# Attention with both heads of a pair in one weighted-sum batch, ahead of a mixture of experts and a dense layer

## The chip, the cores and the metric

The kernel runs on one core of a Trainium2 chip. A core has five engines that work side by side, each through its own queue in order: TensorE (matrix products; the trace lists its weight loads apart, as PEld), VectorE (DVE), ScalarE (ACT), GpSimd (POOL) and SyncE (SP), which here issues DMA transfers. The metric is the device time of one execution in microseconds (us); a figure for a kernel is the median of several runs.

## What is computed

Attention runs on two batches of eight heads, 768 tokens, 64 numbers per head. Queries and keys are given the nearest of 16 centroids of their head, and a query sees only keys of its own cluster. Its output goes through a mixture of eight experts (each token to the one expert with the largest logit) and then through a dense layer with a gated activation. Only attention and the two products that stand right behind it (the logits of the expert choice and of the output gate) are touched by the change.

```python
q_assign = argmax(einsum('bhsd,hcd->bhsc', q_n, c_n), -1)      # k_assign alike
mask = q_assign[:, :, :, None] == k_assign[:, :, None, :]
scores = where(mask, scale * q @ k.T, -1e9)
attn = exp(scores - max(scores, -1))
attn_out = (attn / (sum(attn, -1) + 1e-9)) @ v
x = attn_out.transpose(0, 2, 1, 3).reshape(B * S, H * D)
logits = x @ w_gate;  e_idx = argmax(logits, 1);  eom = sigmoid(x @ w_output_gate)
# x -> expert e_idx (relu(x @ w1[e]) @ w2[e], weighted) -> (g(x @ w_in)) @ w_out
```

## The kernel before

Attention is cut into eight units, a unit being a batch and a pair of heads; a unit has 12 steps, a step being 128 queries of one head against all 768 keys. So there are 96 steps, `i` in the loop, and r = 0 to 11 within a unit. All instructions are issued in an order written out by hand, so each engine takes its work in exactly the order of the program.

Pass `i` of the loop does, in this order: `prepare(i, True)` (pieces marked early); `emit_scores(i + 1)`, four TensorE products into one of two PSUM buffers (L419, L420) and the maximum on VectorE (L422); in every third pass one waiting output product, `ostage` (L474, L476); `prepare(i)`, other pieces of the next unit; one waiting weighted-sum batch, `weighted` (L459, L462, L464, L465); `emit_pt(i - 1)`, the transposes of the exponentials in two halves, each half with one PSUM buffer of its own, copied out by ScalarE (first half, L441) and by VectorE (second half, L443), with routing work spread between the halves; `emit_exp(i + 1)` on ScalarE (L428).

A weighted-sum batch covers one head and three steps: six blocks of 128 keys, each in two column groups of 32, even and odd blocks in different quarters of the array, so that four products run at once; every product is two instructions, as the numbers are 32 bits wide. Even and odd sums stay in two halves of the partitions, and the output product adds them: its moving matrix `wo` has, in each half, the unit matrix and that head's rows of the two gate matrices (80 columns). VectorE scales the product by the reciprocal of the sums of exponentials and puts it into `xw`. Batches are queued two passes after their last step; in a unit they run at r = 5, 8, 11 and at r = 2 of the next one, their output products one pass later. In all units but the last the steps go through one head and then through the other.

While a unit runs, the next one is prepared in nine pieces, at the passes that `plan_at` gives relative to the first step of the running unit (-3, -2, 0, 1, 3, 5, 6, 7, 8; for unit 1 the first two at 0): transposes of queries and keys, for each head (`pqk`, L256, in the one PSUM buffer that the batches use, too; high part by ScalarE, low part by VectorE, L260; six DMAs for the queries and six for the keys); cluster scores of both (`pcl`, L326, in the PSUM buffer of the output products) with a block transpose (L330) and the first maximum and comparisons on VectorE (L300 to L302); second maximum (L309); one-hots (L314); their block transpose (L334) with the rows of ones (L338, eight DMAs). Inputs of unit u + 2 are loaded at r = 9 of unit u - 1 (for unit 2 at pass 3). `setup_rest` fills `wo` ahead of the first pass. When the last output product of a batch's tokens is done, `route` picks the experts and scatters the rows; the expert stage follows.

Of the kernel before, what the change touches and what calls it, by code (L numbers as in the profile page):

```python
# [9 lines left out]
F32 = mybir.dt.float32  # L10
# [3 lines left out]
AF = mybir.ActivationFunctionType  # L14
ALU = mybir.AluOpType
# [4 lines left out]
B, H, S, D = 2, 8, 768, 64  # L20
C = 16
NT = B * S
DM = H * D
E = 8
DFF = 2048
T = S // 128
XW = 80
# [12 lines left out]
def tile_t(j):  # L40

    return 2 * (j % 3) + j // 3
# [3 lines left out]
def attention_moe_ffn(ctx: ExitStack, tc: tile.TileContext, q, k, v, centroids, w_gate, w_og, w1, w2, w_in, w_out, out):  # L46
    nc = tc.nc
# [6 lines left out]
    ident = const.tile([128, 128], F32, name="ident")  # L54
# [38 lines left out]
    at = ExitStack()  # L93
    ld = at.enter_context(tc.tile_pool(name="ld", reuse_waits="tile", bufs=2))
    one = at.enter_context(tc.tile_pool(name="one", reuse_waits="tile", bufs=1))
    stk = at.enter_context(tc.tile_pool(name="stk", reuse_waits="tile", bufs=2))
    pp = at.enter_context(tc.tile_pool(name="pp", reuse_waits="tile", bufs=4))
    ptp = at.enter_context(tc.tile_pool(name="ptp", reuse_waits="tile", bufs=2))
    xwp = at.enter_context(tc.tile_pool(name="xwp", reuse_waits="tile", bufs=1))
    xw = [xwp.tile([128, T, H, XW], F32, name=f"xw{b}") for b in range(B)]  # L100
    ps_s = at.enter_context(tc.tile_pool(name="ps_s", reuse_waits="tile", bufs=2, space=PSUM))
# [6 lines left out]
    oh_scale = one.tile([128, 1], F32, name="oh_scale")  # L108
    oh_bias = one.tile([128, 1], F32, name="oh_bias")
    nought = one.tile([128, 1], F32, name="nought")  # L110
    wo = one.tile([128, H, XW], F32, name="wo")
    tri = one.tile([128, 128], BF16, name="tri")
    ones = one.tile([128, 128], BF16, name="ones")

# [1 line left out]
    st = {}  # L116
# [74 lines left out]
    def setup_rest():  # L191

        blocks = f32(cblk).rearrange("p h (x r) c -> p h x (r c)", x=2)
        nc.gpsimd.tensor_tensor(cfull, blocks[:, :, 0], blocks[:, :, 1], op=ALU.add)
        nc.gpsimd.memset(oh_scale[0:64], 1.0)
        nc.gpsimd.memset(oh_scale[64:128], BIG)
        nc.gpsimd.memset(oh_bias[0:64], 0.0)
        nc.gpsimd.memset(oh_bias[64:128], -BIG)
        for r in range(2):
            rows = slice(64 * r, 64 * r + 64)  # L200
            nc.gpsimd.tensor_copy(wo[rows, :, 0:D], ident[rows, None, rows].to_broadcast([64, H, D]))
            nc.sync.dma_start(out=wo[rows, :, D:D + E], in_=w_gate.rearrange("(h d) e -> d h e", h=H))
            nc.sync.dma_start(out=wo[rows, :, D + E:XW], in_=w_og.rearrange("(h d) e -> d h e", h=H))
        t32 = one.tile([128, 128], F32, name="t32")
        nc.gpsimd.memset(t32, 1.0)
        nc.gpsimd.tensor_copy(ones, t32)
        nc.gpsimd.affine_select(out=t32, in_=t32, pattern=[[1, 128]], compare_op=ALU.is_gt, fill=0.0, base=0, channel_multiplier=-1)
        nc.gpsimd.tensor_copy(tri, t32)
        nc.gpsimd.tensor_copy(rev8, rev16[:, C - E:])
        ei = one.tile([128, E], I32, name="ei")  # L210
        nc.gpsimd.iota(ei, [[NT, E]], base=0, channel_multiplier=0)
        nc.gpsimd.tensor_copy(ebase, ei)
        nc.gpsimd.tensor_scalar(iota8, ebase, 1.0 / NT, None, op0=ALU.mult)
        for e in range(E):
# [22 lines left out]
    def prep_pieces(u):  # L237
# [148 lines left out]
        if u == 0:  # L386
# [3 lines left out]
            ]  # L390
        return [
            [transposes("q", 0)], [transposes("q", 1), stacks("q")], [transposes("k", 0)], [transposes("k", 1), stacks("k")],
            [], [scores, by_token, argmax_a], [argmax_b], [chosen], [by_cluster, rows_of_ones],
        ]


# [1 line left out]
    TAIL, WAITS = 3, (3, 2, 0)  # L398
    steps = [(u, h, j) for u in range(len(UNITS)) for h in range(2) for j in range(T)]

    steps[-2 * T:] = sorted(steps[-2 * T:], key=lambda s_: s_[2] // 3)
    NS = len(steps)
    live = {}

    def emit_scores(i):
        u, h, j = steps[i]
        d = st[u]
        L = live[i] = {}
        if j % 3 == 0:
            L["sm"] = pp.tile([128, 3], F32, name="sm", tag="sm")  # L410
            L["pT"] = ptp.tile([128, T, 384], F32, name="pT", tag="pT")
        else:
            for nm in ("sm", "pT"):
                L[nm] = live[i - 1][nm]
        sp = L["sp"] = ps_s.tile([128, 2, 512], F32, name="sp", tag="sp")
        cs = slice(j * 128, (j + 1) * 128)
        for n in range(2):
            ks = slice(384 * n, 384 * n + 384)
            nc.tensor.matmul(sp[:, n, :384], d["Q1"][:, h, cs], d["X"][:, h, ks], start=True, stop=False)  # L419
            nc.tensor.matmul(sp[:, n, :384], d["Q2"][:, h, cs], d["Z"][:, h, ks], start=False, stop=True)  # L420
        nm = L["nm"] = pp.tile([128, 1], F32, name="nm", tag="nm")
        nc.vector.tensor_reduce(nm, sp[:, :, :384], op=ALU.max, axis=AX.XY, negate=True)  # L422

    def emit_exp(i):
        L = live[i]
        j = steps[i][2]
        P = L["P"] = pp.tile([128, 2, 384], F32, name="P", tag="P")
        nc.scalar.activation(P, L["sp"][:, :, :384], AF.Exp, bias=L["nm"], accum_out=L["sm"][:, j % 3:j % 3 + 1])  # L428

    def emit_pt(i):  # L430
        L = live[i]
        j = steps[i][2]
        for n in range(2):
# [9 lines left out]
                nc.vector.tensor_copy(dst, src)  # L443
            advance(2)

    av = deque()
    ost = deque()

    def queue_av(i):
        u, h, j = steps[i]  # L450
        L = live[i]
        hold = {}

        def weighted():
            po = ps_a.tile([128, 512], F32, name="po", tag="po")
            for kt in range(T):
                for a in range(2):
                    g = 2 * (kt % 2) + a
                    nc.tensor.matmul(po[32 * g:32 * g + 32, :384], st[u]["v"][:, h, tile_t(kt), 32 * a:32 * a + 32],  # L459
                                     L["pT"][:, kt, :], start=kt < 2, stop=kt >= T - 2)  # L460
            oa = hold["oa"] = pp.tile([128, 384], F32, name="oa", tag="oa")
            nc.scalar.copy(oa, po[:, :384])  # L462
            rs = hold["rs"] = pp.tile([128, 3], F32, name="rs", tag="rs")
            nc.vector.tensor_scalar(rs, L["sm"], 1e-9, None, op0=ALU.add)  # L464
            nc.vector.reciprocal(rs, rs)  # L465
            ost.append(ostage)

        def ostage():
            b, pr = UNITS[u]
            hh = 2 * pr + h  # L470
            po = ps_m.tile([128, 512], F32, name="pox", tag="m")
            pv = po[:, :3 * XW].rearrange("p (r c) -> p r c", r=3)
            for r in range(3):
                nc.tensor.matmul(pv[:, r], hold["oa"][:, r * 128:(r + 1) * 128], wo[:, hh], start=True, stop=True)  # L474
            j0 = j - 2
            nc.vector.tensor_tensor(xw[b][:, j0:j0 + 3, hh, :], pv, hold["rs"][:, :, None].to_broadcast([128, 3, XW]), op=ALU.mult)  # L476
            if (hh, j0) == (H - 1, 0) and b == B - 1:
                routing.append(route(1))

        av.append(weighted)  # L480


# [181 lines left out]
            nc.vector.tensor_tensor(ci[:, b], t2, place[b], op=ALU.add)  # L664


    plan_at = {}
    for u in range(1, len(UNITS)):
        for n, r in enumerate((-3, -2, 0, 1, 3, 5, 6, 7, 8) if u > 1 else (0, 0, 0, 1, 3, 5, 6, 7, 8)):
            plan_at.setdefault((12 * (u - 1) + r, n == 6), []).append((u, n))  # L670
    pieces = {}

    def prepare(i, early=False):
        for u, n in plan_at.get((i, early), ()):
            if u not in pieces:
                pieces[u] = prep_pieces(u)
            for f in pieces[u][n]:
                f()

    with tc.manual_schedule():  # L680
# [14 lines left out]
        for i in range(NS + 2):  # L695
            nu, r = divmod(i + 3, 12)
            if i == 3 or r == 0 and nu + 2 < len(UNITS):
                load_unit(nu + 2)
            prepare(i, True)
            if i + 1 < NS:  # L700
                emit_scores(i + 1)
            tail = i >= NS - TAIL
            if (tail or i % 3 == 0) and ost:
                ost.popleft()()
            prepare(i)
            if i == 0:
# [527 lines left out]
```

## Time and profile before

| | us |
|---|---|
| median of 3 runs (744.11 to 746.38) | 746.01 |
| the profiled execution, time | 743.06 |
| its span, first to last instruction | 741.4 |
| TensorE busy in the span | 715.3 (96%) |
| VectorE busy | 476.1 (64%) |
| ScalarE busy | 391.6 (53%) |
| GpSimd busy | 221.4 (30%) |
| mean granted TensorE clock | 0.986 |

An engine's busy share is a mean over stages with different limits; attention is roughly the first 260 us of the span. Matrix products are pipelined, so their durations overlap: what one costs is read from start to start, not from its duration. The trace names what an idle engine waited for.

### The profile page before, as it was taken

To read this page: it belongs to the slowest core of one execution; us is meant where nothing else is said; L and a number is where in the kernel's file an instruction comes from. 1 tells how busy PE (TensorE), PEld (TensorE's weight loads), DVE (VectorE), ACT (ScalarE), POOL (GpSimd) and SP (SyncE) were. 2 spreads that over 40 slices of the span, in tenths; PEclk is the share of its full clock that TensorE was granted. 3 is DMA by queue.
4 is the path that set the end of the run, shared out by engine and by line. 5 is a ranking of instruction groups with operands and counts; after the bars stand their busy time and mean duration, and the time that the engine had idled before them with its cause. 6 is when DMAs were issued, how large, how long until landed. Compare 5 with 4: busy or idle time off the path is not lost.

```text
span 741.4 us, 12821 instructions
## 1 busy us (share of the span) xinstructions
PE 715.3 (96%) x4698; PEld 587.8 (79%) x4698; DVE 476.1 (64%) x918; ACT 391.6 (53%) x784; POOL 221.4 (30%) x161
## 2 busy tenths in 40 slices
PE   8999999999999978999989988999999999999996
PEld 5777777777777758999989888877888888888885
DVE  5878788788887761665667766787545656232322
ACT  3766666666666634557767676544434344222120
POOL 3000000000700035757778887222332212020202
PEclk8999999999999989999999999999999999999998
DMA  8765948538340049756676673232643211010101
GB/s 235 177 187 154 238 161 258 128 82 199 97 128 13 1 154 326 246 179 221 206 256 216 217 252 141 85 114 86 70 68 40 79 58 57 0 58 0 58 1 57
DMA packets 66243, 98.28 MB, mean 133 GB/s; under 512 B 9248, under 2 KB 44960, under 8 KB 66176
## 3 DMA queue, kind: packets, MB, share of 16 engines
q1 hardware_dynamic: 63872, 91.12, 43.1%
q0 software_dynamic: 2304, 6.30, 2.3%
q8 instruction: 38, 0.62, 0.4%
q14 instruction: 29, 0.24, 0.1%
HBM read 64.46 MB, written 12.59 MB: 104 GB/s over the span
## 4 chain that ended last, share of the span: by engine, by line
PE 27%; issue 16%; DVE 9%; ACT 5%; POOL 3%; DMA 2%; POOLq 0%; SPq 0%; ACTq 0%; DVEq 0%
PE ph L1064 3%; PE ph L1063 3%; PE ph L1062 3%; PE py L1156 3%; PE py L1155 3%; PE py L1154 3%; ACT w L786 2%; DMA xr<-xd 2%; DVE w L789 1%; PE py L886 1%; PE ph L886 1%; DVE ct L824 1%; DVE ph L893 1%; POOL out_dram L1164 1%; PE py L884 1%
## 5 line engine op out<-in xcount | busy, mean ns | idle before, releaser
L789 POOL TENSOR_TENSOR w<-raw,w 128x1024 fp32r<-128x1024 f32 x47 | 117.5, 2514 | 34.8 <-ACT w L786 32.0
L1139 DVE TENSOR_TENSOR sg<-ph,sg 128x512 f32<-128x512 f32 x48 | 33.2, 691 | 103.6 <-ACT sg L1138 103.2
L422 DVE TENSOR_REDUCE nm<-sp 128x1 f32<-128x768 f32 x96 | 91.3, 952 | 9.6 <-PE sp L420 8.4
L428 ACT ACTIVATE P<-sp,nm 128x768 f32<-128x768 f32 x96 | 87.1, 907 | 5.2 <-DVE nm L422 5.0
L1138 ACT ACTIVATE sg<-ph 128x512 f32<-128x512 f32 x48 | 28.7, 598 | 108.7 <-PE ph L1064 105.4
L836 POOL TENSOR_TENSOR w<-csq,w 128x512 fp32r<-128x512 f32 x32 | 43.5, 1360 | 137.0 <-ACT w L835 137.0
L436 PEld LDWEIGHTS pt<-ident,P 128*128 128x128 f32 x576 | 65.1, 143 | 21.3 <-issue 19.4
L436 PE MATMUL pt<-ident,P 128*128 128x128 f32 x576 | 81.2, 276 | 0.3 <-DVE pT L443 0.2
L1063 PE MATMUL ph<-ytl,w 128*128 128x512 f32 x192 | 76.1, 397 | 0.0
L1062 PE MATMUL ph<-yth,w 128*128 128x512 f32 x192 | 76.0, 396 | 0.0
L1064 PE MATMUL ph<-yth,w 128*128 128x512 f32 x192 | 75.6, 394 | 0.1
L1155 PE MATMUL py<-w,gh 128*128 128x512 f32 x192 | 75.3, 392 | 0.0
L1156 PE MATMUL py<-w,gl 128*128 128x512 f32 x192 | 75.2, 391 | 0.0
L1154 PE MATMUL py<-w,gh 128*128 128x512 f32 x192 | 74.9, 390 | 0.0
L419 PE MATMUL sp<-X,Q 128*128 128x384 f32 x192 | 73.5, 383 | 0.5 <-ACT P L428 0.4
L786 ACT CAST w<-raw 128x1024 fp32r<-128x1024 f32 x64 | 66.8, 1044 | 7.7 <-DMA raw<-in_moe_w_dram 7.6
L443 DVE COPY pT<-pt 128x384 f32<-128x384 f32 x96 | 52.8, 550 | 27.5 <-PE pt L436 27.1
L886 PE MATMUL py<-ht,w 128*128 128x480 f32 (+5 forms) x192 | 61.8, 373 | 7.0 <-DVE room L893 5.2
L459 PE MATMUL po<-pT,ld_v 128*32 128x384 f32 x768 | 68.4, 489 | 0.2 <-ACT pT L441 0.2
L420 PE MATMUL sp<-Z,Q 80*128 80x384 f32 x192 | 65.3, 340 | 0.5 <-DMA Z<-Hk 0.5
L886 PE MATMUL ph<-t,w 128*128 128x480 f32 (+5 forms) x192 | 61.1, 370 | 1.5 <-DVE ht L910 1.5
L585 POOL TENSOR_SCALAR xs<-xw,gate 128x512 f32<-128x512 f32 x6 | 9.9, 1643 | 174.6 <-DVE gate L567 174.2
(233 smaller groups left out, 1559.0 us busy)
## 6 DMA issues: line engine op xcount, KB each, us to landing
raw<-in_moe_w_dram SPq DMA_DIRECT2D x64, 512.0 KB, 4.0
raw<-in_moe_w_in_dram SPq DMA_DIRECT2D x16, 512.0 KB, 4.6
raw<-in_moe_w_out_dram SPq DMA_DIRECT2D x16, 512.0 KB, 3.6
Q<-Hq SPq DMA_DIRECT2D x32, 192.0 KB, 5.8
xd<-zrow SPq DMA_DIRECT2D x8, 768.0 KB, 6.9
ld_q<-in_q_dram SPq DMA_DIRECT2D x8, 384.0 KB, 3.6
ld_k<-in_k_dram SPq DMA_DIRECT2D x8, 384.0 KB, 4.9
ld_v<-in_v_dram SPq DMA_DIRECT2D x8, 384.0 KB, 6.1
```

The costliest lines, as they stand in the source:

```text
L422: nc.vector.tensor_reduce(nm, sp[:, :, :384], op=ALU.max, axis=AX.XY, negate=True)
L428: nc.scalar.activation(P, L["sp"][:, :, :384], AF.Exp, bias=L["nm"], accum_out=L["sm"][:, j % 3:j % 3 + 1])
L436: nc.tensor.transpose(pt[:, r * 128:(r + 1) * 128], L["P"][:, n, r * 128:(r + 1) * 128], ident)
L786: nc.scalar.copy(hi, r)
L789: (eng or nc.gpsimd).tensor_tensor(lo, r, f32(hi), op=ALU.subtract)
L886: nc.tensor.matmul(ps[:, :2 * n], w_hi, t, start=first, stop=False)
L1062: nc.tensor.matmul(ph, wa(key, 0, k, i), yth[:, k, cs], start=(k == 0), stop=False)
L1063: nc.tensor.matmul(ph, wa(key, 0, k, i), ytl[:, k, cs], start=False, stop=False)
L1064: nc.tensor.matmul(ph, wa(key, 1, k, i), yth[:, k, cs], start=False, stop=(k == 3))
L1154: nc.tensor.matmul(po[m], gh[:, ms], wb(key, 0, i), start=first, stop=False)
L1155: nc.tensor.matmul(po[m], gh[:, ms], wb(key, 1, i), start=False, stop=False)
L1156: nc.tensor.matmul(po[m], gl[:, ms], wb(key, 0, i), start=False, stop=last)
```

## The change

Units 1 to 7 go through the steps of both heads by thirds: three steps of head 0, three of head 1, three more of each (as the last unit did before). From unit 1 on, except for the second half of unit 7, one batch serves both heads: its four column groups hold two heads times two halves of the head's width, and all six blocks of keys add into the same groups. It is issued in two parts of three blocks, in two passes (r = 8 and 9, and r = 2 and 3 of the next unit), and gives one output product of 160 columns, with one copy, one reciprocal and one scaling for both heads; that product comes at r = 0 and 6. `wo` becomes wider, with zeros in the half of the other head; a second matrix `wl` keeps the old form for unit 0 and the end of unit 7, so that twelve small DMAs fill both in place of four. Four buffers hold transposed exponentials in place of two.

The plan of the pieces moves: for units 2 and on the cluster scores go from r = 5 to r = 2, the second maximum from 6 to 3, the one-hots from 7 to 3; for units 3 and on the queries are transposed at -2 and -1. For every unit the cluster scores now come behind the batch of their pass (before, ahead of it), and the block transpose of the one-hots goes with the one-hots.

```diff
-    ptp = at.enter_context(tc.tile_pool(name="ptp", reuse_waits="tile", bufs=2))
+    ptp = at.enter_context(tc.tile_pool(name="ptp", reuse_waits="tile", bufs=4))
-    wo = one.tile([128, H, XW], F32, name="wo")
+    wo = one.tile([128, H // 2, 2, XW], F32, name="wo")
+    wl = one.tile([128, 2, 2, XW], F32, name="wl")
+        nc.gpsimd.memset(wo, 0.0)
         for r in range(2):
             rows = slice(64 * r, 64 * r + 64)
-            nc.gpsimd.tensor_copy(wo[rows, :, 0:D], ident[rows, None, rows].to_broadcast([64, H, D]))
-            nc.sync.dma_start(out=wo[rows, :, D:D + E], in_=w_gate.rearrange("(h d) e -> d h e", h=H))
-            nc.sync.dma_start(out=wo[rows, :, D + E:XW], in_=w_og.rearrange("(h d) e -> d h e", h=H))
+            nc.gpsimd.tensor_copy(wo[rows, :, r, 0:D], ident[rows, None, rows].to_broadcast([64, H // 2, D]))
+            nc.gpsimd.tensor_copy(wl[rows, :, :, 0:D], ident[rows, None, None, rows].to_broadcast([64, 2, 2, D]))
+            for n, w in enumerate((w_gate, w_og)):
+                cs = slice(D + E * n, D + E * n + E)
+                by_head = w.rearrange("(p r d) e -> r d p e", r=2, d=D)
+                nc.sync.dma_start(out=wo[rows, :, r, cs], in_=by_head[r])
+                for m, d0 in enumerate((0, DM - 2 * D)):
+                    nc.sync.dma_start(out=wl[rows, m, :, cs], in_=w[d0:d0 + 2 * D].rearrange("(h d) e -> d h e", h=2))
-            [], [scores, by_token, argmax_a], [argmax_b], [chosen], [by_cluster, rows_of_ones],
+            [], [scores, by_token, argmax_a], [argmax_b], [chosen, by_cluster], [rows_of_ones],
-    steps[-2 * T:] = sorted(steps[-2 * T:], key=lambda s_: s_[2] // 3)
+    steps[2 * T:] = sorted(steps[2 * T:], key=lambda s_: (s_[0], s_[2] // 3))
+    KTS = (range(0, 3), range(3, T))
 ...
+        alone = u == 0 or i >= NS - T
+        heads = (h,) if alone else (0, 1)
+        if len(heads) == 2 and h == 0:
+            return
+        pts = [live[i]["pT"]] if alone else [live[i - 3]["pT"], live[i]["pT"]]
+        def products(kts):
 ...
+            for kt in kts:
+                for n, hh in enumerate(heads):
+                    for a in range(2):
+                        g = 2 * (kt % 2 if alone else n) + a
+                        nc.tensor.matmul(po[32 * g:32 * g + 32, :384], v_[:, hh, tile_t(kt), 32 * a:32 * a + 32],
+                                         pts[n][:, kt, :], start=kt < (2 if alone else 1), stop=kt >= T - (2 if alone else 1))
         def weighted():
+            products(KTS[-1] if not alone else range(T))
 ...
-                nc.tensor.matmul(pv[:, r], hold["oa"][:, r * 128:(r + 1) * 128], wo[:, hh], start=True, stop=True)
+                nc.tensor.matmul(pv[:, r], hold["oa"][:, r * 128:(r + 1) * 128], wl[:, int(u > 0), h] if alone else wo[:, pr], start=True, stop=True)
+        if not alone:
+            for kts in KTS[:-1]:
+                av.append(lambda kts=kts: products(kts))
         av.append(weighted)
+    PLAN = ((0, 0, 0, 1, 3, 5, 6, 7, 8), (-3, -2, 0, 1, 1, 2, 3, 3, 8), (-2, -1, 0, 1, 1, 2, 3, 3, 8))
-        for n, r in enumerate((-3, -2, 0, 1, 3, 5, 6, 7, 8) if u > 1 else (0, 0, 0, 1, 3, 5, 6, 7, 8)):
-            plan_at.setdefault((12 * (u - 1) + r, n == 6), []).append((u, n))
+        for n, r in enumerate(PLAN[min(u, 3) - 1]):
+            plan_at.setdefault((12 * (u - 1) + r, n == 6, n == 5), []).append((u, n))
                 if av:
                     av.popleft()()
+            prepare(i, False, True)
             if 0 <= i - 1 < NS:
                 emit_pt(i - 1)
```

## Rows read from the trace of the kernel before

**Rows 1.** Busy time by stretch: stretch, length, PE, PEld, DVE, ACT, POOL busy; clock, DMA

```profile
44.22:74.73 30.51, 30.51 (x271) 22.85 (x270) 24.91 (x48) 20.49 (x46) 0.00 (x0) 1.00 0.65 175
166.30:197.00 30.70, 30.70 (x275) 22.92 (x274) 26.91 (x68) 20.47 (x48) 8.36 (x6) 1.00 0.54 141
```

**Rows 2.** Timeline of TensorE, unit 1 from step 5: start, length, line, operation, count

```profile
59.71 0.52 PE L326 MATMUL pcl<-Hq,cfull 128*32 128x384 f32 x2
...
61.03 2.12 PE L459 MATMUL po<-pT,ld_v 128*32 128x384 f32 x24
63.08 0.87 PE L436 MATMUL pt<-ident,P 128*128 128x128 f32 x6
63.71 0.42 PE L419 MATMUL sp<-X,Q 128*128 128x384 f32 x1
...
64.51 0.79 PE L474 MATMUL pox<-wo,oa 128*128 128x80 f32 x6
65.13 0.82 PE L436 MATMUL pt<-ident,P 128*128 128x128 f32 x6
65.71 0.42 PE L419 MATMUL sp<-X,Q 128*128 128x384 f32 x1
...
67.09 0.44 PE L419 MATMUL sp<-X,Q 128*128 128x384 f32 x1
...
67.98 2.14 PE L459 MATMUL po<-pT,ld_v 128*32 128x384 f32 x24
```

**Rows 3.** Timeline of TensorE, unit 0: plain steps 2 to 4, and step 9

```profile
25.19 0.42 PE L419 MATMUL sp<-X,Q 128*128 128x384 f32 x1
...
28.29 0.44 PE L419 MATMUL sp<-X,Q 128*128 128x384 f32 x1
...
41.59 0.49 PE L256 MATMUL pqk<-ident,ld_q 128*128 128x128 f32 x3
```

**Rows 4.** Timeline of VectorE, unit 0, the maximum of the scores issued at 25.19

```profile
26.19 0.96 DVE L422 TENSOR_REDUCE nm<-sp 128x1 f32<-128x768 f32 x1
```

**Rows 5.** Timeline of TensorE, expert stage, first and last of thirteen products of 320 columns

```profile
304.17 0.31 PE L882 MATMUL py<-ht,w 128*128 128x320 f32 x1
...
305.93 0.31 PE L882 MATMUL ph<-t,w 128*128 128x320 f32 x1
```

**Rows 6.** Timeline of VectorE, unit 1, steps 5 to 8

```profile
61.28 0.58 DVE L330 STREAM_TRANSPOSE sc<-pcl 128x384 f32<-128x384 f32 x1 [0.43 <-PE pcl L326]
...
63.55 0.16 DVE L464 TENSOR_SCALAR rs<-sm 128x3 f32<-128x3 f32 x1
...
63.99 0.56 DVE L443 COPY pT<-pt 128x384 f32<-128x384 f32 x1
...
64.92 0.95 DVE L422 TENSOR_REDUCE nm<-sp 128x1 f32<-128x768 f32 x1
65.78 0.40 DVE L476 TENSOR_TENSOR xw<-pox,rs 128x240 f32<-128x240 f32 x1
66.10 0.55 DVE L443 COPY pT<-pt 128x384 f32<-128x384 f32 x1
...
67.65 0.55 DVE L314 TENSOR_TENSOR oh<-eq,m 128x384 bf16<-128x384 f32 x1
68.11 0.55 DVE L443 COPY pT<-pt 128x384 f32<-128x384 f32 x1
...
69.44 0.56 DVE L334 STREAM_TRANSPOSE oT<-oh 128x384 bf16<-128x384 bf16 x1
69.94 0.12 DVE L464 TENSOR_SCALAR rs<-sm 128x3 f32<-128x3 f32 x1
```

**Rows 7.** Timeline of SyncE's DMA queue, first load of a gate matrix, load of unit 2's queries

```profile
20.32 0.68 SPq L202 DMA_DIRECT2D wo<-in_moe_w_gate_dram  x1
...
33.51 0.76 SPq L127 DMA_DIRECT2D ld_q<-in_q_dram  x1
```

**Rows 8.** That load of queries by its tile: time from issue to landing

```profile
DMA to landing us min/median/max: 4.7/4.7/4.7
```

More of the change, by code (lines that the diff above doesn't have):

```diff
@@ L408, in emit_scores @@
         L = live[i] = {}
+        L["sm"] = live[i - 1]["sm"] if i % (6 if u else 3) else pp.tile([128, 2, 3], F32, name="sm", tag="sm")
         if j % 3 == 0:
-            L["sm"] = pp.tile([128, 3], F32, name="sm", tag="sm")
             L["pT"] = ptp.tile([128, T, 384], F32, name="pT", tag="pT")
         else:
-            for nm in ("sm", "pT"):
-                L[nm] = live[i - 1][nm]
+            L["pT"] = live[i - 1]["pT"]
         sp = L["sp"] = ps_s.tile([128, 2, 512], F32, name="sp", tag="sp")
@@ L425, in emit_exp @@
         L = live[i]
-        j = steps[i][2]
+        _, h, j = steps[i]
         P = L["P"] = pp.tile([128, 2, 384], F32, name="P", tag="P")
-        nc.scalar.activation(P, L["sp"][:, :, :384], AF.Exp, bias=L["nm"], accum_out=L["sm"][:, j % 3:j % 3 + 1])
+        nc.scalar.activation(P, L["sp"][:, :, :384], AF.Exp, bias=L["nm"], accum_out=L["sm"][:, h, j % 3:j % 3 + 1])
     def emit_pt(i):
@@ L450, in queue_av @@
         u, h, j = steps[i]
-        L = live[i]
-        hold = {}
-        def weighted():
[L455 to L460, printed above, removed]
-            oa = hold["oa"] = pp.tile([128, 384], F32, name="oa", tag="oa")
[L462 to L465, printed above, removed]
+        b, pr = UNITS[u]
@@ new lines, in queue_av @@
+        v_ = st[u]["v"]
+        j0 = j - 2
+        alone = u == 0 or i >= NS - T
[3 more added lines that the diff above has]
+        pts = [live[i]["pT"]] if alone else [live[i - 3]["pT"], live[i]["pT"]]
+        sums = live[i]["sm"]
+        hold = {}
+        def products(kts):
+            if "po" not in hold:
+                hold["po"] = ps_a.tile([128, 512], F32, name="po", tag="po")
+            po = hold["po"]
+            for kt in kts:
[4 more added lines that the diff above has]
+                                         pts[n][:, kt, :], start=kt < (2 if alone else 1), stop=kt >= T - (2 if alone else 1))
@@ L466, in weighted @@
+        def weighted():
+            products(KTS[-1] if not alone else range(T))
+            oa = hold["oa"] = pp.tile([128, 384], F32, name="oa", tag="oa")
+            nc.scalar.copy(oa, hold["po"][:, :384])
+            rs = hold["rs"] = pp.tile([128, 2, 3], F32, name="rs", tag="rs")
+            hs = slice(heads[0], heads[-1] + 1)
+            nc.vector.tensor_scalar(rs[:, hs], sums[:, hs], 1e-9, None, op0=ALU.add)
+            nc.vector.reciprocal(rs[:, hs], rs[:, hs])
             ost.append(ostage)
@@ L468, in ostage @@
         def ostage():
-            b, pr = UNITS[u]
-            hh = 2 * pr + h
+            n = len(heads)
+            hh = 2 * pr + heads[0]
             po = ps_m.tile([128, 512], F32, name="pox", tag="m")
-            pv = po[:, :3 * XW].rearrange("p (r c) -> p r c", r=3)
+            pv = po[:, :3 * n * XW].rearrange("p (r h c) -> p r h c", r=3, h=n)
             for r in range(3):
-                nc.tensor.matmul(pv[:, r], hold["oa"][:, r * 128:(r + 1) * 128], wo[:, hh], start=True, stop=True)
@@ L475, in ostage @@
-            j0 = j - 2
-            nc.vector.tensor_tensor(xw[b][:, j0:j0 + 3, hh, :], pv, hold["rs"][:, :, None].to_broadcast([128, 3, XW]), op=ALU.mult)
-            if (hh, j0) == (H - 1, 0) and b == B - 1:
+                nc.tensor.matmul(pv[:, r], hold["oa"][:, r * 128:(r + 1) * 128], wl[:, int(u > 0), h] if alone else wo[:, pr], start=True, stop=True)
+            scale = hold["rs"][:, heads[0]:heads[-1] + 1].rearrange("p h r -> p r h")
+            nc.vector.tensor_tensor(xw[b][:, j0:j0 + 3, hh:hh + n, :], pv, scale[:, :, :, None].to_broadcast([128, 3, n, XW]), op=ALU.mult)
@@ L478, in ostage @@
+            if (pr, j0) == (H // 2 - 1, 0) and b == B - 1:
                 routing.append(route(1))
+        if not alone:
+            for kts in KTS[:-1]:
+                av.append(lambda kts=kts: products(kts))
         av.append(weighted)
@@ L664, in place_ids, with prepare @@
             nc.vector.tensor_tensor(ci[:, b], t2, place[b], op=ALU.add)
+    PLAN = ((0, 0, 0, 1, 3, 5, 6, 7, 8), (-3, -2, 0, 1, 1, 2, 3, 3, 8), (-2, -1, 0, 1, 1, 2, 3, 3, 8))
     plan_at = {}
     for u in range(1, len(UNITS)):
-        for n, r in enumerate((-3, -2, 0, 1, 3, 5, 6, 7, 8) if u > 1 else (0, 0, 0, 1, 3, 5, 6, 7, 8)):
-            plan_at.setdefault((12 * (u - 1) + r, n == 6), []).append((u, n))
+        for n, r in enumerate(PLAN[min(u, 3) - 1]):
+            plan_at.setdefault((12 * (u - 1) + r, n == 6, n == 5), []).append((u, n))
     pieces = {}
-    def prepare(i, early=False):
-        for u, n in plan_at.get((i, early), ()):
+    def prepare(i, early=False, late=False):
+        for u, n in plan_at.get((i, early, late), ()):
             if u not in pieces:
```

## Prediction, on record before the changed kernel was run

> **What bounds the kernel now.** I read the busy times by stretch first. In a whole unit of attention TensorE is busy for all of its 30.51 us, VectorE for 24.91 and ScalarE for 20.49; GpSimd does nothing [rows 1]. So from unit 1 on, each microsecond taken from TensorE is gained, and each that TensorE must wait is lost, whatever the other engines' averages say. Next I read the order of TensorE and VectorE side by side, to get prices from start to start (in microseconds): transposes 0.58 (65.13 to 65.71), a plain step 1.38 (65.71 to 67.09), hence scores 0.80; scores ahead of a batch 0.89; a batch 2.05; transposes after it 0.63; an output product 0.62; cluster scores plus batch 3.37, of which the cluster scores are 1.32 [rows 2]. No wait stands in these rows: extra TensorE work lies between any two plain steps. Last I looked where TensorE does run plain steps in a row: in unit 0, where two of them take 28.29 - 25.19 = 3.10, not 2.76 [rows 3]. That is the loop scores, maximum, exponential, score buffer free again; the maximum starts 1.00 after the scores [rows 4], so from its start to the next scores but one it takes 2.10.
>
> **What is gained.** Thirteen pairs of batches (two in each of units 1 to 6, one in unit 7) become thirteen merged ones of the same 48 matmul instructions, so the sums cost the same: two parts of 2.05, two entries and two exits of the packed form, as before. The output product falls from twelve instructions of 80 columns to six of 160. At 80 columns they follow each other at 0.62 / 6 = 0.103 us [rows 2]. The expert matmuls stream 320 columns in one pass at 0.147 ((305.93 - 304.17) / 12), each with a weight load of its own [rows 5]; 160 columns in the two-pass format are as many passes of a column, so I take 6 x 0.147 = 0.88, against 2 x 0.62 = 1.24: 0.36 saved, times 13 = 4.7 us. Bounds: with the spacing still 0.103, 0.62 x 13 = 8.1; with no load hidden (0.103 + 0.147 / 2 = 0.177), 0.18 x 13 = 2.3. I take the middle, since the expert rows have the same load and stream.
>
> A rule that speaks against this: the Trainium skill (TensorE: Matmul & The Clock Gate, Back-to-back issue gap) gives an isolated matmul N / 2.4 + 2.5 ns, which for 160 column passes is 69 ns; by that alone columns set the price, the change moves no column, and nothing is saved. The same section says that in a stream with weight loads both set the spacing, and the measured 103 ns sides with that.
>
> Thirteen copies of the sum (ScalarE) and reciprocals and scalings of half the count (VectorE) go, too. I cost that at nothing: both engines have idle time in the average [rows 1].
>
> **What the moved preparation costs.** The cluster scores were in step 5, ahead of a batch, and their VectorE chain (block transpose, argmax) ran beside 2.05 us of batch; copies of step 5 came after both. For units 2 on they come in step 2, behind a part. Queued on VectorE behind the chain are the copy of the transposes of step 1, the second maximum, the maximum of step 4's scores, the one-hots, their block transpose, the reciprocals and the copy of step 2; TensorE's transposes wait for those copies, since each half has one buffer.
>
> A steady unit, from the start of step 2's scores (0): part at 0.89, cluster scores after it, transposes at 0.89 + 3.37 = 4.26, next scores 4.89, second part 5.78, transposes 7.83, scores 8.46, transposes 9.26, their second half 0.29 later, at 9.55. VectorE: the block transpose starts 1.57 after the cluster scores do [rows 2, 6], here about 4.4 (4.25 to 4.5). Four operations take 2.27 (61.28 to 63.55): copy at 6.67; copy and second maximum 0.93: maximum at 7.60; 0.86: one-hots at 8.46; 0.46: block transpose at 8.92; 0.50: reciprocals at 9.42; two of them 0.3: copy at 9.72, done at 9.72 + 0.55 = 10.27 [rows 6]. TensorE wants that buffer at 9.55 and gets it at 10.3: 0.74 lost. Next late is the maximum behind the copy (10.19): the scores two steps on can't start before 10.19 + 2.10 = 12.29, TensorE would be there at 10.3 + 0.29 + 1.38 = 11.97: 0.32. Together 1.06, and even without a late copy the two plain steps 4 and 5 cost 3.10 - 2.76 = 0.34.
>
> Unit 1 is worse: the batch in its step 2 is a whole one of unit 0, so step 3 has an output product (0.62) and no second part. By the same working the second halves wait 0.67 (step 3) and 1.69 (step 4), then 0.30 for the exponential, and steps 6 and 7 are plain, too (0.34): 3.0. Unit 0 keeps its plan, but its cluster scores also go behind the batch, in step 5, because the new third place takes every unit's: waits of 0.67 (step 6) and 0.73 (step 7, behind the second maximum, the maximum and the 0.32 of the scaling): 1.4. Unit 5 holds the routing of the first 768 tokens, 2.0 us more of VectorE [rows 1]; in between I take 1.2 of it (0 to 2.0): 2.25. Unit 6 ends with two plain steps, as unit 7 has no successor to prepare: 0.34; unit 7 has its own pair: 0.34.
>
> SyncE: twelve small loads of the gate weights in place of four. One takes 0.68 of its queue [rows 7], so the queue is 5.3 us later (4.8 to 7) by the load of unit 2's queries: issued at 33.51 + 5.3, landing 4.7 after that [rows 7, 8], at 43.5. TensorE wants them at 41.59 [rows 3], by then 1.4 later, 43.0: 0.5 lost (0 to 2.6). Behind it stand the other two loads and the ones' DMAs, wanted later. The memset of the wide weights is hidden on GpSimd, idle then; the extra buffers cost space only. Transposing the queries one step later puts four such steps in a row (10, 11, 0, 1), in each of which VectorE has 0.86 + 0.47 + 0.47 and TensorE 1.38 and a product of three; that lags by about 0.1 a step and an output product in step 0 makes up for it: nothing, up to 0.8 a unit where the one PSUM buffer of these transposes comes late. The tail: routing of the last batch's first half starts one step later, mostly beside the last batch: 0.3 (0 to 1).
>
> Sum: unit 0 1.4, load 0.5, unit 1 3.0, units 2, 3, 4 and 6 4 x 1.06 = 4.2, unit 5 2.25, 0.34 twice, tail 0.3: 12.3 lost; 4.7 gained; net 7.6 us slower. The profiled execution took 743.06 (span 741.4 and 1.66 around it), which gives 750.7; the median of the runs shown, 746.01, stands 2.95 above it, so I forecast **753.6 us** in those terms.
>
> **The rivals.** *The chain fits* (same): block transpose to copy is 5.9 us of VectorE against 5.2 of TensorE, so 0.7 less, by a shorter pipeline between operations than these rows show, and only the plain pairs cost (units 1 to 7: 0.34 x 7, another in unit 1, one at the end of 6), with the load 1.9 and the tail 0.3: 5.3 lost, 4.7 gained, 746.6 us. For it: the chain misses by under a microsecond. Against: units 0 and 1 miss by far more.
>
> *It does what it says* (faster): no wait, and the product at 4.7 to 8.1: 738 to 741.3 us. This needs the plain steps not to cost, and the rows of unit 0 say that they do. It decides against me if TensorE shows no wait in step 4 of a unit.
>
> *The backlog carries on* (slower still): four query and key steps lag, 0.8 in each of five units, 4 more: 757.6 us.
>
> *Columns set the product's price* (slower still): nothing gained, 746.0 + 12.3 = 758.3 us. The Trainium skill's isolated gap (above) is this rival's rule; the measured spacing speaks against it.
>
> **How the numbers follow.** Chances: forecast 0.60, carried backlog 0.12, no gain by columns 0.03, chain fits 0.15, as it says 0.10. The slower three make 0.75, the same 0.15, the faster 0.10 (0.3% is about what a measurement of this kernel can tell from no change). The range takes in the slower cases, with the price bounds, and the case of the chain that fits: 745.0 to 758.5; left out are the faster case and what lies beyond the ends. The slower cases' own range is 749 to 758.5.
>
> **What would show it.** Right: TensorE waits of 0.6 to 0.9 us in the second half of step 4's transposes, released by the copy to pT on VectorE, in units 2 to 6, of about 1.7 in unit 1; then one of 0.3 at scores, released by the exponential; a period of a steady unit of 30.5 - 0.7 + 1.1 = 30.9; output products of 160 columns at 0.15 us spacing; the load of unit 2's queries issued 5 us later. Wrong: a period under 30.2 us, TensorE busy without such waits, or a block transpose of the cluster scores that starts well before the transposes of its step.

## The result, and the profile after

| | before | after |
|---|---|---|
| median, us | 746.15 (744.11 to 746.38) | 753.23 (752.70 to 754.50) |
| the profiled execution, us (span) | 743.06 (741.4) | 754.50 (752.8) |
| TensorE busy, us (share) | 715.3 (96%) | 716.1 (95%) |
| VectorE busy, us (share) | 476.1 (64%) | 469.4 (62%) |

The changed kernel takes 1.0101 times as long as the kernel before, 95% interval 1.0084 to 1.0118: 7.1 us more by the medians (6.3 to 8.8 by the interval), where 7.6 were forecast. The median of the kernel before is now that of four runs; the forecast was put on that of the first three, 746.01. In the profiled executions TensorE is busy for 0.8 us more in a span that is 11.4 us longer: nearly all that is added is time in which it idles. The first view of after is the list of TensorE's waits in attention, from 33 to 268 us (us in total, times, longest):

```profile
PE pt L442 <- ACT pT L447: 5.5, 8, 1.1
PE pt L442 <- DVE pT L449: 1.2, 2, 0.8
PE sp L426 <- DMA Q<-ohT: 0.7, 1, 0.7
```

In after the scores stand at L425 and L426, the maximum at L428, the transposes at L442, their two copies at L447 (ScalarE) and L449 (VectorE), the batch at L477, the output product at L496, the cluster scores at L333, their block transpose at L337, the one-hots and theirs at L321 and L341. The busy times of a steady unit answer to [rows 1], from cluster scores to cluster scores:

```profile
90.14:120.98 30.84, 30.20 (x261) 21.84 (x256) 23.99 (x41) 19.70 (x43) 0.00 (x0) 1.00 0.69 199
```

TensorE is no longer busy throughout: 30.20 of 30.84 us. The timeline of TensorE in that unit shows where, from the cluster scores on (one row for each kind where several follow):

```profile
90.14 0.49 PE L333 MATMUL pcl<-Hq,cfull 128*32 128x384 f32 x2
...
91.54 0.87 PE L442 MATMUL pt<-ident,P 128*128 128x128 f32 x6
...
95.14 0.87 PE L442 MATMUL pt<-ident,P 128*128 128x128 f32 x6
...
96.56 0.49 PE L442 MATMUL pt<-ident,P 128*128 128x128 f32 x3
97.62 0.55 PE L442 MATMUL pt<-ident,P 128*128 128x128 f32 x3 [0.57 <-ACT pT L447]
...
98.71 0.84 PE L442 MATMUL pt<-ident,P 128*128 128x128 f32 x6
99.62 0.44 PE L425 MATMUL sp<-X,Q 128*128 128x384 f32 x1
...
100.44 0.98 PE L496 MATMUL pox<-wo,oa 128*128 128x160 f32 x6
101.25 0.82 PE L442 MATMUL pt<-ident,P 128*128 128x128 f32 x6
```

A half of transposes that waits for nothing gives the engine to the other 0.29 later; here it takes 97.62 - 96.56 = 1.06, so 0.77 is lost. The next scores come 99.62 - 98.71 = 0.91 after their transposes where 0.58 is usual: another 0.33. The two make 1.10 us a unit. VectorE in the same stretch, from the block transpose of the cluster scores to the copy and the maximum behind it:

```profile
91.68 0.58 DVE L337 STREAM_TRANSPOSE sc<-pcl 128x384 f32<-128x384 f32 x1 [2.27 <-PE pcl L333]
...
93.95 0.55 DVE L449 COPY pT<-pt 128x384 f32<-128x384 f32 x1
94.42 0.54 DVE L316 TENSOR_REDUCE m<-eq 128x24 f32<-128x384 f32 x1
94.88 0.95 DVE L428 TENSOR_REDUCE nm<-sp 128x1 f32<-128x768 f32 x1
95.75 0.55 DVE L321 TENSOR_TENSOR oh<-eq,m 128x384 bf16<-128x384 f32 x1
96.33 0.58 DVE L341 STREAM_TRANSPOSE oT<-oh 128x384 bf16<-128x384 bf16 x1
...
97.10 0.52 DVE L449 COPY pT<-pt 128x384 f32<-128x384 f32 x1
97.54 0.95 DVE L428 TENSOR_REDUCE nm<-sp 128x1 f32<-128x768 f32 x1
```

VectorE is idle for 2.27 us ahead of 91.68, because it waits for the cluster scores, and then has no gap until the last row: the copy of transposes issued at 95.14 starts at 97.10. The engine with 24 busy microseconds in 30.84 is the one that is late. The trace puts the wait itself down to ScalarE's copy of the first half; the last experiment takes that up.

### The profile page after: what moved, and what is told of

It is laid out like the page before. It is cut to its first block, busy times and chain, and to the rows that moved or that the text cites. A ratio compares the mean times of both kernels' runs of the same rounds, so it can differ in the third digit from the quotient of the medians.

```text
span 752.8 us, 12581 instructions
## 1 busy us (share of the span) xinstructions
PE 716.1 (95%) x4620; PEld 583.0 (77%) x4620; DVE 469.4 (62%) x879; ACT 387.1 (51%) x771; POOL 221.5 (29%) x164
## 4 chain that ended last, share of the span: by engine, by line
PE 29%; issue 16%; DVE 9%; ACT 5%; POOL 3%; DMA 0%; POOLq 0%; ACTq 0%; SPq 0%; DVEq 0%
PE ph L1091 3%; PE ph L1090 3%; PE ph L1089 3%; PE py L1183 3%; PE py L1182 3%; PE py L1181 3%; ACT w L813 2%; PE ph L913 1%; PE py L913 1%; DVE w L816 1%; DVE ct L851 1%; PE ph L910 1%; DVE ph L920 1%; PE ph L909 1%; PE py L911 1%
## 5 line engine op out<-in xcount | busy, mean ns | idle before, releaser
L428 DVE TENSOR_REDUCE nm<-sp 128x1 f32<-128x768 f32 x96 | 91.5, 953 | 14.3 <-PE sp L426 13.2
L442 PE MATMUL pt<-ident,P 128*128 128x128 f32 x576 | 83.8, 277 | 7.1 <-ACT pT L447 5.7
L442 PEld LDWEIGHTS pt<-ident,P 128*128 128x128 f32 x576 | 65.2, 141 | 31.4 <-issue 17.5
L425 PE MATMUL sp<-X,Q 128*128 128x384 f32 x192 | 74.6, 389 | 2.7 <-DMA X<-Lk 2.3
L449 DVE COPY pT<-pt 128x384 f32<-128x384 f32 x96 | 52.6, 548 | 29.2 <-PE pt L442 29.1
L477 PE MATMUL po<-pT,ld_v 128*32 128x384 f32 x768 | 68.6, 490 | 0.0
L426 PE MATMUL sp<-Z,Q 80*128 80x384 f32 x192 | 66.6, 347 | 0.7 <-DMA Q<-ohT 0.7
L447 ACT COPY pT<-pt 128x384 f32<-128x384 f32 x96 | 45.7, 476 | 38.7 <-PE pt L442 38.5
```

What stands on the lines that cost most here:

```text
L442: nc.tensor.transpose(pt[:, r * 128:(r + 1) * 128], L["P"][:, n, r * 128:(r + 1) * 128], ident)
```

## The experiments

The chances and the sum rested on one claim, that the chain on VectorE stalls TensorE because the cluster scores stand behind the batch. The experiments undo that alone, do it alone, and then take the other parts one by one. Each ratio is to the kernel before, run on the same chip beside it.

**The cluster scores ahead of the part again.** One change to after:

```diff
-            plan_at.setdefault((12 * (u - 1) + r, n == 6, n == 5), []).append((u, n))
+            plan_at.setdefault((12 * (u - 1) + r, n == 6, False), []).append((u, n))
...
-            prepare(i, False, True)
```

> The changed kernel with one thing undone: the cluster scores stand ahead of the batch or part of their pass, as they did before. Theory (VectorE's chain behind the cluster scores holds up the copies): the chain starts 2.0 us earlier and runs beside the part again. Unit 0 gets back 1.4 us, unit 1 about 1.5, units 2, 3, 4 and 6 0.75 each (the wait of the transposes in step 4 goes, the 0.3 of the two plain steps stays), unit 5 1.2: 7.1 in all, so 746.1 us (744.5 to 748), level with the kernel before. Rival (merging and splitting the batches itself costs, by the four steps without a batch that it leaves): the order within a pass doesn't matter, 752 to 754 us.

Measured 746.67 us (745.38 to 749.95), ratio 1.0026 [1.0010, 1.0041]. The timeline of TensorE, the cluster scores of two units and the plain pair between:

```profile
114.77 0.52 PE L333 MATMUL pcl<-Hq,cfull 128*32 128x384 f32 x2
...
124.53 0.84 PE L442 MATMUL pt<-ident,P 128*128 128x128 f32 x6
125.43 0.44 PE L425 MATMUL sp<-X,Q 128*128 128x384 f32 x1
...
144.82 0.52 PE L333 MATMUL pcl<-Hq,cfull 128*32 128x384 f32 x2
```

The period is 30.05 instead of 30.84 and the second halves of a steady unit wait no longer; of the unit's 1.10 only the plain pair's 0.90 - 0.58 = 0.32 is left. So the place behind the batch costs 1.0101 - 1.0026 = 0.75% of the time, 5.6 us, about three quarters of the loss; 7.1 were expected back, which would have been level with the kernel before. What remains is 1.9 us slower than before (0.7 to 3.1 by the interval), but not in attention: from the scores of step 5 to the last output product it takes 234.77 us, where before took 235.40. In this trace the merged batches pay a little even with the plain pair; the rest is lost where the experts begin (below, what stays open).

**The place alone, in the kernel before.**

```diff
-            plan_at.setdefault((12 * (u - 1) + r, n == 6), []).append((u, n))
+            plan_at.setdefault((12 * (u - 1) + r, n == 6, n == 5), []).append((u, n))
...
+            prepare(i, False, True)
             if 0 <= i - 1 < NS:
                 emit_pt(i - 1)
```

> The kernel before with that one thing alone: the cluster scores go behind the batch of step 5; nothing is merged and no piece moves. Theory: in each of units 0 to 6 the transposes' second halves wait about 0.7 us in step 6 and 0.7 in step 7, 1.4 x 7 = 9.8 us: 756 us. Rival (merging and splitting costs): no change, 745 to 747 us.

Measured 754.37 us (753.77 to 756.19), ratio 1.0118 [1.0092, 1.0144]. Two rows of TensorE, of a pair that comes in each of units 0 to 6 (L441 is ScalarE's copy here, L443 VectorE's):

```profile
100.93 0.55 PE L436 MATMUL pt<-ident,P 128*128 128x128 f32 x3 [0.57 <-ACT pT L441]
...
102.92 0.55 PE L436 MATMUL pt<-ident,P 128*128 128x128 f32 x3 [0.40 <-DVE pT L443]
```

With no other part of the change, the place makes a loss as large as that of the whole change. It is not the same loss: behind a whole batch in step 5 two second halves wait in each unit, 0.57 + 0.40 of idle time, and a unit is 31.90 long in place of 30.51. Attention is 9.9 us longer in this trace, as forecast; the time is longer by 1.18%, 8.8 us. The rival, by which the place makes no difference, falls.

**Eight of the twelve gate loads later.** After, with only the four loads that unit 0 needs ahead of the first pass:

```diff
+    def gate_loads(late):
...
+                if late:
+                    nc.sync.dma_start(out=wo[rows, :, r, cs], in_=by_head[r])
+                m, d0 = ((0, 0), (1, DM - 2 * D))[late]
+                nc.sync.dma_start(out=wl[rows, m, :, cs], in_=w[d0:d0 + 2 * D].rearrange("(h d) e -> d h e", h=2))
...
+            if i == 12:
+                gate_loads(1)
```

> The changed kernel with eight of the twelve small loads of the gate weights issued at pass 12 and not ahead of the first pass. Theory: the load of unit 2's queries (0.3 us waited in the trace) and the DMAs of the rows of ones (0.7 us waited at the scores of pass 11) come in time: 1.0 us less, 752.2 us. Rival (the queue of loads also explains the late first scores, 2.6 us in the profile of the changed kernel): 3.6 us less, 749.6 us.

Measured 751.93 us (750.98 to 752.43), ratio 1.0088 [1.0068, 1.0108]. SyncE's queue, the load of unit 2's queries in after, and the wait of TensorE's scores for the ones' DMAs behind it:

```profile
39.42 0.82 SPq L128 DMA_DIRECT2D ld_q<-in_q_dram  x1
```

```profile
49.43 0.42 PE L426 MATMUL sp<-Z,Q 80*128 80x384 f32 x1 [0.68 <-DMA Q<-ohT]
```

and the same load with the loads later:

```profile
33.95 0.55 SPq L128 DMA_DIRECT2D ld_q<-in_q_dram  x1
```

The queue's delay is the loads': 5.5 us between the two rows, of which the first gate load makes 0.3 (20.95 and 20.62). The wait for the ones' DMAs is gone. The time moved by 0.13%, 1.0 us, as expected, but the two intervals overlap, so that the times alone do not show it. Nor does the trace: the last experiment keeps the early loads, has no such wait either, and its attention is as long (241.33 us, here 241.31; after 242.60). The loads cost up to 1.0 us in some executions, and not in every one. TensorE's waits for X and Z at the very start of attention are not the gate loads' doing: in after the last of them ends at 19.91, ahead of the first gate load at 20.95.

**The chain covered.** Four changes at once, for a version that keeps what pays: the loads of the last experiment; cluster scores ahead of a part; the two parts in steps 2 and 4, so that no two plain steps follow each other behind the chain; and the first half of unit 1 by head, with unit 2 prepared on the old plan (the lines on the loads and on the place of the cluster scores, as in the diffs above, are left out, and so is the third pair of heads in `wl`):

```diff
...
-        alone = u == 0 or i >= NS - T
+        alone = i < 2 * T + T or i >= NS - T
...
-    PLAN = ((0, 0, 0, 1, 3, 5, 6, 7, 8), (-3, -2, 0, 1, 1, 2, 3, 3, 8), (-2, -1, 0, 1, 1, 2, 3, 3, 8))
+    PLAN = ((0, 0, 0, 1, 3, 5, 6, 7, 8), (-3, -2, 0, 1, 3, 5, 6, 7, 8), (-2, -1, 0, 1, 1, 2, 3, 4, 8))
...
-                if av:
+                if av and (i < 24 or i % 12 != 3):
                     av.popleft()()
...
```

> The merged batches with what theory says they need: cluster scores ahead of the part; a pair's two parts in steps 2 and 4 (the one-hots and their block transpose with the second), so that no two plain steps follow each other there; unit 1's first half not merged and its successor prepared by the old plan; eight of the loads (now twelve of sixteen) at pass 12. Theory: twelve merged output products save 0.43 us each (0.81 us in the trace of the changed kernel against 2 x 0.62), 5.2 us, and some 0.6 is lost where unit 6 ends with plain steps and in the last unit: 741.5 us (740 to 744), under the kernel before. Rival (merging and splitting itself costs): 746 us or more.

Measured 743.03 us (740.96 to 745.20), ratio 0.9968 [0.9953, 0.9984]: faster than both kernels. TensorE, one unit with its first output product:

```profile
114.33 0.52 PE L339 MATMUL pcl<-Hq,cfull 128*32 128x384 f32 x2
...
125.50 0.98 PE L502 MATMUL pox<-wo,oa 128*128 128x160 f32 x6
126.32 0.82 PE L448 MATMUL pt<-ident,P 128*128 128x128 f32 x6
...
144.07 0.52 PE L339 MATMUL pcl<-Hq,cfull 128*32 128x384 f32 x2
```

The period is 29.74, 0.77 below before's 30.51 [rows 1]; TensorE's list of waits in the steady units is empty. The merged product pays once nothing waits.

**Its output products by head again.** The version above, with each product of 160 columns issued as two of 80:

```diff
-                nc.tensor.matmul(pv[:, r], hold["oa"][:, r * 128:(r + 1) * 128], wl[:, min(u, 2), h] if alone else wo[:, pr], start=True, stop=True)
+                for m in range(n):
+                    nc.tensor.matmul(pv[:, r, m], hold["oa"][:, r * 128:(r + 1) * 128], wl[:, min(u, 2), h] if alone else wo[:, pr, m], start=True, stop=True)
```

> The version with the chain covered, but each merged batch's output product as two products of 80 columns from the same copied sums, into the same buffer; copies, reciprocals, scalings and everything else stay merged. Theory (the whole gain of merging is the wider product, 0.81 us against 2 x 0.62): 12 x 0.43 = 5.2 us slower, 748.2 us, and 1.0070 of that version. Rival (the gain lies in the halved copies and scalings, or in fewer stages): no slower than 744 us.

Measured 746.36 us (744.73 to 748.81), ratio 1.0020 [1.0006, 1.0033].

```profile
123.91 1.46 PE L503 MATMUL pox<-wo,oa 128*128 128x80 f32 x12
125.21 0.82 PE L448 MATMUL pt<-ident,P 128*128 128x128 f32 x6
```

Twelve products of 80 columns take 125.21 - 123.91 = 1.30 (0.108 each), six of 160 took 126.32 - 125.50 = 0.82 (0.136 each). The period is 30.71 (cluster scores at 112.74 and 143.45), 0.97 more, twice 0.48: the product's price is where the version's gain is from, and it comes through to the end. The times differ by 0.52%, 3.9 us, where 5.2 were expected; with these intervals 1.6 to 6.0. Attention alone is 5.7 us longer (236.56 against 230.91); 2.5 of it is given back between attention and the experts, where this execution does not have the loss told of below.

**Its parts in steps 2 and 3 again.** The version above, with the parts and the one-hots where after has them:

```diff
-    PLAN = ((0, 0, 0, 1, 3, 5, 6, 7, 8), (-3, -2, 0, 1, 3, 5, 6, 7, 8), (-2, -1, 0, 1, 1, 2, 3, 4, 8))
+    PLAN = ((0, 0, 0, 1, 3, 5, 6, 7, 8), (-3, -2, 0, 1, 3, 5, 6, 7, 8), (-2, -1, 0, 1, 1, 2, 3, 3, 8))
...
-                if av and (i < 24 or i % 12 != 3):
+                if av:
```

> The version with the chain covered, but the two parts of each pair in adjacent steps again (2 and 3), and the one-hots with their block transpose in step 3. Theory (two plain steps in a row take 3.10 us and not 2.76): steps 4 and 5 are plain again in units 2 to 7, 0.34 x 6 = 2.0 us slower, 745.0 us, with a period of a steady unit of 30.05 against 29.74 us. Rival (only the VectorE chain ever made waits): no change, 743 us and a period of 29.74.

Measured 744.09 us (741.51 to 745.39), ratio 0.9987 [0.9974, 1.0001].

```profile
123.79 0.83 PE L448 MATMUL pt<-ident,P 128*128 128x128 f32 x6
124.69 0.44 PE L431 MATMUL sp<-X,Q 128*128 128x384 f32 x1
```

The plain pair is back, 0.90 - 0.58 = 0.32, and the period is 30.04 (cluster scores at 114.02 and 144.06). The trace shows the step's price as expected; the time moved by 0.19%, within what the intervals leave open.

**Own buffers for the two halves.** The waits of after are put down to ScalarE's copy, where I had named VectorE's. In unit 1 they can be told apart. TensorE, ScalarE and VectorE of after:

```profile
65.34 0.49 PE L442 MATMUL pt<-ident,P 128*128 128x128 f32 x3
66.91 0.55 PE L442 MATMUL pt<-ident,P 128*128 128x128 f32 x3 [1.08 <-ACT pT L447]
```

```profile
66.39 0.47 ACT L447 COPY pT<-pt 128x384 f32<-128x384 f32 x1
```

```profile
66.72 0.52 DVE L449 COPY pT<-pt 128x384 f32<-128x384 f32 x1
```

The second half starts 0.05 after ScalarE's copy ends (66.86), while VectorE's, of the step before, runs until 67.24. So it cannot have been put where VectorE still read. In the code the two halves share two buffers of one tag, in the kernel before as in after; that each half has one of its own, as I had written and reckoned, is wrong. These second halves start when ScalarE has copied the first half of the same step, as if they had been given its buffer. The experiment gives each half its own:

```diff
-    ps_t = at.enter_context(tc.tile_pool(name="ps_t", reuse_waits="tile", bufs=2, space=PSUM))
+    ps_t = at.enter_context(tc.tile_pool(name="ps_t", reuse_waits="tile", bufs=1, space=PSUM))
...
-            pt = ps_t.tile([128, 512], F32, name="pt", tag="pt")
+            pt = ps_t.tile([128, 512], F32, name="pt", tag=f"pt{n}")
```

> The changed kernel with one PSUM buffer of its own for each half of the transposes (a separate tag for each, one buffer each), where both halves took turns in two buffers of one tag; nothing else. In the changed kernel the stalled second halves start 0.05 us after ScalarE's copy of the first half of the same step (66.91 in unit 1, while VectorE's copy of the step before ends only at 67.24), as if they were handed that half's buffer. Theory: VectorE's backlog sets the wait all the same, since its copy comes as late as the other buffer; then the stalled second halves are released by VectorE's copy, a steady unit's wait stays at 0.7 to 0.85 us and its period at 30.8 to 30.95, in unit 1 the first wait falls to about 0.65 and the second grows to 1.6 from 1.28, and the time is that of the changed kernel, 752.5 to 754 (1.009 to 1.012 of the kernel before). Rival: the turn-taking in two buffers is itself the loss; then with own buffers the second halves of a steady unit start with a wait under 0.3 us, the period falls to 30.3 or below, and the time to 748 to 749.5.

Measured 753.13 us (752.49 to 754.41), ratio 1.0115 [1.0082, 1.0148]. TensorE, the two waits of unit 1 and that of a steady unit:

```profile
63.38 0.55 PE L442 MATMUL pt<-ident,P 128*128 128x128 f32 x3 [0.47 <-DVE pT L449]
...
64.48 0.49 PE L442 MATMUL pt<-ident,P 128*128 128x128 f32 x3
66.54 0.55 PE L442 MATMUL pt<-ident,P 128*128 128x128 f32 x3 [1.56 <-DVE pT L449]
...
126.63 0.49 PE L442 MATMUL pt<-ident,P 128*128 128x128 f32 x3
127.75 0.55 PE L442 MATMUL pt<-ident,P 128*128 128x128 f32 x3 [0.63 <-DVE pT L449]
```

All these waits are now VectorE's. The steady wait hardly changes (127.75 - 126.63 - 0.29 = 0.83, where after has 0.77), nor does the time. So VectorE's backlog alone makes a wait of this size, and sharing the buffers is not the loss. In after itself ScalarE's copy ends the wait, and in a steady unit VectorE's ends at the same moment (97.10 + 0.52 = 97.62). Why the two come out alike is not shown.

## Why the prediction was right, point by point

The forecast was 753.6 us, and the experiments show its mechanism, but for the copy that ends the waits. That the net came so close, 7.1 for 7.6, is in part luck: attention lost more than was forecast (13.6 for 12.3 us), it gained more (6.4 for 4.7), and some 2 us were lost outside attention, for which there was no term. By its own steps:

- **Steady units.** 0.74 and 0.32 were forecast, 0.77 and 0.33 measured; the period 30.84 against 30.9. The 0.77 ends with another copy than the working had, so that a part of the agreement is chance; with own buffers, as the working had it, 0.83 was measured. The price of the plain pair, 0.34 by unit 0 of before [rows 3], held to two hundredths in after and in the two experiments that have a plain pair.
- **Unit 0.** Forecast 1.4; 0.77 and 0.61 measured, 1.38.
- **Unit 1.** Forecast 3.0 in parts of 0.67, 1.69, 0.30 and 0.34; measured 3.07, but in other parts: 0.77 (64.24), 1.28 (66.91), 0.67 and 0.35. The step that failed is the one that gives each half a buffer of its own, which these two steps of after do not have. With own buffers the two waits are 0.67 and 1.77, close to the working. The total is the same because what the half did not wait for, the scores two steps on did: the maximum behind VectorE's copy is as late.
- **The releaser.** Named as VectorE's copy; in after it is ScalarE's in eight of ten waits. With own buffers it is VectorE's, as told above.
- **Unit 5.** Forecast 2.25. Two second halves idle for 1.01 and 0.83 and their starts come 1.34 and 1.03 late, with six small routing products inside the first; 0.20 at the scores behind them: 2.4 to 2.6.
- **The load of unit 2's queries.** SyncE's queue is later by the forecast 5.3 (39.42 against 33.51 [rows 7], in an execution whose first gate load is 0.6 later). Of the cost of 0.5 the step counted one wait; the ones' DMAs, which stand behind that load and which I called wanted later, cost 0.68 more, so about 1.0. The execution with own buffers, whose load is nearly as late (38.76), has neither wait: this term is 0 to 1.0.
- **The output product.** The mis-sized term: forecast 0.88 for six of 160 columns, measured 101.25 - 100.44 = 0.81, or 0.135 each; the saving is 1.24 - 0.81 = 0.43 a pair, 5.6 us for thirteen, not 4.7. The expert rows [rows 5], 0.147, were the nearest rows but not the same form.
- **The four query and key steps in a row** were costed at nothing, up to 0.8 a unit. About 0.09 is left for them: 30.84 is that much above 30.51 - 2 x 0.43 + 1.10.
- **The rule that was to speak against the change.** By the Trainium skill (TensorE: Matmul & The Clock Gate, Back-to-back issue gap) an isolated matmul takes N / 2.4 + 2.5 ns: for 320 column passes (160 columns, twice) an estimate of 136 ns. The trace agrees: 0.135 us at 160 columns. At 80 columns that rule gives 69 ns, and the trace has 0.103 to 0.108, so that there something else sets the price. By the same section it is the weight load as well, which no run here takes apart. So the rival's rule holds for the wide product and not for the narrow one, and that is why something was gained.
- **A gain that was missed.** In before, one output product, at the seam of the two batches, waited for ScalarE's copy of the sum. Two rows of before's TensorE, this one and the last output product:

```profile
133.23 0.90 PE L474 MATMUL pox<-wo,oa 128*128 128x80 f32 x6 [0.57 <-ACT oa L462]
...
263.69 0.90 PE L474 MATMUL pox<-wo,oa 128*128 128x80 f32 x6 [0.60 <-ACT oa L462]
```

The unit with the first of them is 31.35 long, not 30.51; in after that wait is gone: 0.84 gained. The list of before's waits has it, and no term of the sum did.

**The sum closes in attention.** From the scores of step 5 to the last output product it was 263.69 - 28.29 = 235.40 us [rows 3]; the same two of after:

```profile
30.67 0.44 PE L425 MATMUL sp<-X,Q 128*128 128x384 f32 x1
...
273.27 0.90 PE L496 MATMUL pox<-wl,oa 128*128 128x80 f32 x6 [0.60 <-ACT oa L483]
```

These are 242.60 apart: 7.2 more. The terms as measured: 1.38 + 1.0 + 3.07 + 4 x 1.10 + 2.5 + 0.65 (two plain pairs, in units 6 and 7) + 0.2 (tail) + 4 x 0.09 = 13.6 lost, 5.6 + 0.84 = 6.4 gained, net 7.2. The 0.09 and the tail are what the other terms leave over, so that the sum closes in part by construction; that the price of the waits and of the product is right, the experiments show.

**What stays open** is outside attention. The profiled execution of after is 11.4 us longer than that of before, 4.2 of it outside this stretch: the scores of step 5 come 2.4 later, and the first expert product comes 17.26 behind the counts of the routing (before, 15.04). The second of these can be read off TensorE's rows, of before and then of after. They are the products on `identb` that are to keep TensorE busy, and the transposes of the gathered rows:

```profile
277.42 1.29 PE L1077 MATMUL ph<-identb 128*128 128x128 bf16 x20 [2.08 <-issue]
279.38 0.66 PE L870 MATMUL pxt<-ident,xr 128*128 128x128 f32 x4 [0.67 <-DMA xr<-xd]
```

```profile
289.01 2.31 PE L1104 MATMUL ph<-identb 128*128 128x128 bf16 x20 [4.81 <-DMA xr<-xd]
291.12 2.53 PE L897 MATMUL pxt<-ident,xr 128*128 128x128 f32 x12
```

Before has done the twenty products when the rows come, 12.06 behind the counts. In after they start only with the rows, 12.11 behind the counts, and the rows' transposes wait another 2.11 for them. Six of the seven kernels with merged batches have this; the one with its products by head has not, nor have the two without merged batches. The table gives attention (as above), the stretch from its last output product to the first expert product, and the time against before by the ratio, all in us:

| | attention | to the experts | time |
|---|---|---|---|
| before | 235.40 | 18.67 | |
| after | 242.60 | 20.89 | +7.5 |
| scores ahead | 234.77 | 20.76 | +1.9 |
| place alone, in before | 245.26 | 18.79 | +8.8 |
| loads later | 241.31 | 20.91 | +6.6 |
| chain covered | 230.91 | 21.48 | -2.4 |
| its products by head | 236.56 | 19.02 | +1.5 |
| its parts adjacent | 232.46 | 21.02 | -1.0 |
| own buffers | 241.33 | 20.61 | +8.6 |

The two columns together account for each kernel's time to within 2 us, though each is read in one execution. Why these products come late in some kernels was not tried; those lines of the program are the same in all. The start varies between executions; its waits are not the gate loads' doing, and what they are was not tried either.

## What to carry to other kernels

An engine with a fifth of its time idle still sets the end if its work comes as one chain: write out, for the stretch in which a chain runs, what is queued behind it and when the busiest engine wants each of these, and put the chain's start beside work of the busiest engine that needs none of them. A piece that is moved to the other side of a neighbour in the program's order (scores behind a batch instead of ahead of it) can cost more than the fusion beside it brings: here 7.8 us of attention against 5.6. Before merging matrix products, compare their spacing at both widths: here 0.103 us at 80 columns and 0.135 at 160, and the difference to twice the narrow one is all that is gained.

## What the runs showed of the hardware

TensorE's clock in the first scores was not the same in two executions. Rows of before, then of after, by stretch, as in [rows 1]:

```profile
12.00:18.00 6.00, 5.92 (x29) 3.39 (x27) 3.14 (x8) 1.49 (x3) 1.31 (x12) 0.57 0.92 215
18.00:24.00 6.00, 5.02 (x31) 4.12 (x31) 4.26 (x7) 4.82 (x12) 0.00 (x0) 1.00 0.56 108
```

```profile
12.00:18.00 6.00, 3.51 (x21) 2.11 (x19) 2.54 (x7) 2.20 (x4) 1.50 (x15) 0.50 0.91 199
18.00:24.00 6.00, 5.32 (x18) 4.39 (x18) 2.31 (x3) 2.08 (x5) 0.00 (x0) 0.50 0.62 138
```

In before the granted clock was at half, 1.2 GHz, for most of the first stretch, in which TensorE was busy for 5.92 of 6 us, and full, 2.4 GHz, in the second. In after TensorE was busy for 3.51 us of the first stretch, waiting for VectorE's one-hots and then for X, and the clock stayed at half through both stretches, though TensorE was busy for 5.32 us of the second. Half clock has its price: six transposes of queries took 1.48 us there (at 22.15) and 0.82 in before (at 19.68). So in this execution a wait of two microseconds for a DMA stands beside six more at half clock. That the wait is the cause is not shown: with the loads later TensorE was busy for 4.46 us of the first stretch, and the clock was 0.83 and then 1.00; with own buffers for 5.30, and it was 0.67 and then 0.62. That the executions differ in this, and by it in where attention begins, I had not allowed for.
